# A statically planned attention and MLP kernel: a new cost model for ScalarE in its planner, new limits for DVE, and a new rule for the close of a group

## The chip, the cores and the metric

The kernel runs on one core of one Trainium2 chip. The metric is device time in microseconds (us) of one execution; lower is better.

## The reference

```python
def reference(A_x, A_wq, A_wk, A_wv, A_wo, B_x, B_w1, B_w2):
    xn = layernorm(A_x)                       # S=2048 rows, D=512, bf16
    # A: attention, 32 heads of 16 with ONE shared key and value head
    q = xn @ wq ; k = xn @ wk ; v = xn @ wv
    s = softmax(q k^T / 4) v  @ wo            # 32 x 2048 x 2048 exponentials
    # B: MLP, F=1792
    g = silu(silu(xn @ w1) @ w2)
    return A_x + s * g
```

The bulk is 134 million exponentials. One score tile is 128 keys by 512 queries of one head. Four heads and one block of 512 queries make a "group" of 64 tiles; there are 32 groups, 2048 tiles in all.

## The kernel before: the parts that matter

All instructions are laid out by a planner that runs when the program is built. It keeps one clock for each engine, gives each operation an estimated duration and a latency to whoever waits for it, and always lets the engine with the earliest clock choose what to do next. What comes out is a fixed order of instructions for each engine; on the chip each engine is given its instructions in that order, and semaphores enforce the dependencies. **So a number in the cost model never changes how long an instruction takes. It changes the order, and which engine a tile is given to.**

```python
T_P, T_SH, T_TR, T_AF = 600.0, 600.0, 630.0, 51.0   # T_AF: fixed cost of one exponential, ns
T_P64, DV_MIN, T_LIB = 1060.0, 4, 6500.0            # POOL's shift; its library
LEND_LIMIT = 3000.0
TWO_LIMIT = 1500.0
LAT = {   # ns from the end of an operation to the engine that waits
    (PE, AC): 221.0, (PE, DV): 221.0, (PE, PE): 0.0,
    (AC, PE): 402.0, (AC, DV): 390.0, (AC, AC): 250.0, ...
```

A score tile is turned into exponentials in one of two ways:

- ScalarE ("A tile"): one `activation(Exp)` over two or three PSUM banks, planned at `0.8333 * 512 * n + T_AF`. The two sets of three banks alternate, so the score matmuls for one wait until ScalarE has read it two exponentials earlier.
- DVE ("D tile"): a `tensor_scalar` writes the bits of an approximate exponential; four such tiles form a batch, of which POOL (sometimes DVE) makes three shifted copies by integer addition; all four copies are multiplied into PV. A D tile thus costs four PV matmuls, an A tile one.

At each score group the planner decides how many D tiles ride along. With one, ScalarE "lends" its third bank, and its exponential has two banks in place of three:

```python
def dve_backlog():
    return sum(t.dur for t in pl.tasks[DV] if all(p.op is not None for p in t.preds)) \
        + max(0.0, pl.clk[DV] - pl.clk[PE])
...
    bl = dve_backlog()
    want = 2 if bl < TWO_LIMIT else 1
    nd = min(cap, 4 - len(banks), len(need), want)
    if nd < min(want, len(need)) and len(banks) == 3 and bl < LEND_LIMIT:
        nd, lend = nd + 1, True
```

Between score groups TensorE does "column" work: PV rounds, and projections for queries, MLP and output ("jobs"). A round is refused if it would make the next score group late for ScalarE:

```python
    end = pe_start(t, mode) + dur + SWITCH
    if max(ts, end) > max(ts, act_need() - 437.0) + S_TOL:
        pl.clk[PE] = ts            # leave TensorE idle until the banks are free
        return True
...
def start_jobs(t):
    ...
    if jb.pace > progress() + 1e-9:                 # not ahead of its pace
        return
    if n >= NPRO and a_pressure() > (START_Z if jb.kind == "z" else START_H):
        return                                      # not while exponentials pile up for PV
...
    if pr and pr[0] == "go" and (a_pressure() >= PRESS):
        col = ("pv", pr[1])                         # PV goes first only under pressure
    elif jr[0] == "go":
        col = ("job", jr[1])
```

PV accumulates a group in one PSUM bank. When it is complete, DVE transposes the bank out ("the norm", `f_sb`), and only then may the next group's PV begin.

The softmax here doesn't subtract the row's maximum and nothing guards it: scores larger than these inputs give would overflow.

Of the kernel before, what the change touches and what calls it, by code (L numbers as in the profile page):

```python
# [5 lines left out]
ACT = mybir.ActivationFunctionType  # L6
# [11 lines left out]
LOG2E = 1.4426950408889634  # L18


T_P, T_SH, T_TR, T_AF = 600.0, 600.0, 630.0, 51.0
T_P64, DV_MIN, T_LIB = 1060.0, 4, 6500.0
RSQRT_M = float(0x5F1FFFF9)
RSQRT_C = ((-0.703952253, 0.703952253 * 2.38924456), (-0.5, 1.5))

# [9 lines left out]
PE, AC, DV, PO, SP = "PE", "ACT", "DVE", "POOL", "SP"  # L35
ENGINES = (PE, AC, DV, PO, SP)
MM = 216.0
SWITCH, SKEW = 105.0, 10.0
INF = float("inf")
DVE_LIMIT = 4000.0  # L40
MARGIN, MARGIN_END = 16, 28
LEND_LIMIT = 3000.0
TWO_LIMIT = 1500.0
HOLD, Q_LEAD = 1000.0, 3.3

LOW_USE, HIGH_USE, USE_WIN = 0.55, 0.8, 3000.0
# [2 lines left out]
NPA, PRESS = 26, 20  # L49
START_Z, START_H = 8, 14  # L50
# [6 lines left out]
class Task:  # L57
# [9 lines left out]

LAT = {
    (PE, AC): 221.0, (PE, DV): 221.0, (PE, PE): 0.0,
    (AC, PE): 402.0, (AC, DV): 390.0, (AC, AC): 250.0, (AC, PO): 410.0, (AC, SP): 410.0,  # L70
    (DV, PE): 140.0, (DV, AC): 150.0, (DV, DV): 115.0, (DV, PO): 165.0, (DV, SP): 180.0,
    (PO, PE): 120.0, (PO, AC): 120.0, (PO, DV): 120.0, (PO, PO): 90.0, (PO, SP): 120.0,
    (SP, SP): 60.0,
# [188 lines left out]
def bass_recurrent_scan__grouped_kv_mqa__dense_activation_silu__prompt_kernel(  # L262
# [19 lines left out]
    NG = 2 * NO  # L282
# [11 lines left out]
    with ExitStack() as es:  # L294
# [23 lines left out]
        t_sb = sb("t_sb", [P, 2, NQ], BF16)  # L318
# [16 lines left out]
        ps = es.enter_context(nc.psum_tensor([P, 8 * 512], FP32))  # L335
# [6 lines left out]
        def bank(b):  # L342
            return ps[:, b * 512:(b + 1) * 512]

        pl = Planner()
# [67 lines left out]
        a = 0  # L413
        for n in first:
            b = a + n
            tiles = range(a, b)
            g = a // 4
            y, w, h = rstd_sb[:, a:b], var_sb[:, 0, a:b], var_sb[:, 1, a:b]

            def dv(fn, reads, writes, pre):  # L420
                return pl.add(Task(DV, 66.0, fn, reads, writes, g, [pre] if pre is not None else []))
            t = pl.add(Task(DV, 66.0, lambda v, a=a, b=b, w=w: v.tensor_scalar(
                w, mv_sb[:, a:b, 1], LN_EPS, None, op0=ALU.add), [("mv", i) for i in tiles], [("ve", a)], g,
                [aggr[i] for i in tiles]))
            t = dv(lambda v, y=y, w=w: v.tensor_scalar(
                y.bitcast(I32), w.bitcast(I32), -0.5, RSQRT_M, op0=ALU.mult, op1=ALU.add), [("ve", a)], [("rs", a)], t)
            for it, (c0, c1) in enumerate(RSQRT_C):
                t = dv(lambda v, y=y, h=h, c0=c0: v.scalar_tensor_tensor(
                    out=h, in0=y, scalar=c0, in1=y, op0=ALU.mult, op1=ALU.mult), [("rs", a)], [("vh", a)], t)
                t = dv(lambda v, w=w, h=h: v.tensor_tensor(h, h, w, ALU.mult), [("ve", a), ("vh", a)], [("vh", a)], t)  # L430
# [8 lines left out]
            a = b  # L439
# [25 lines left out]
        def mk_T(tiles, bk=None):  # L465
            n, t0 = len(tiles), tiles[0]

            def rnd(b):
                def emit(pe, b=b):
                    dst = bank(b).bitcast(BF16).rearrange("p (t d) -> p t d", d=D)  # L470
                    h = None
                    for k, t in enumerate(tiles):
                        for dc in range(NDC):
                            h = pe.transpose(dst[:, k, dc * P:(dc + 1) * P], xn_sb[:, t % 4, dc * P:(dc + 1) * P], ident[:, :])  # L474
                    return h
                return emit

            def consume(jb, op):
                b = jb.bank
                src = bank(b).bitcast(BF16)[:, 0:n * D].rearrange("p (t c d) -> p c t d", c=NDC, d=P)  # L480
                dst = xnT_sb[:, :, t0 * P:(t0 + n) * P].rearrange("p c (t d) -> p c t d", d=P)
                keys = [("xnT", t) for t in tiles]
                if bk is not None and t0 != 1:
                    return [Task(AC, 477.0, lambda a: a.activation(dst, src, ACT.Copy), [("ps", b)], keys, 0)]
                return [Task(DV, 60.0 + 267.0 * n, lambda v: v.tensor_copy(dst, src), [("ps", b)], keys, 0)]

            job("T", tiles, 0.0, [(rnd, [("xn", t % 4) for t in tiles] + [("id", i) for i in range(4)], 4 * n * T_TP)], consume,
                preds=[xn_task[t] for t in tiles], bk=bk, mode="F")
# [84 lines left out]
        def mk_h(c, ft, pace):  # L573
            def rnd(dc):
                def mk(b):
                    return lambda pe: col4(pe, b, lambda j: w1_sb[:, dc, P * ft + 32 * j:P * ft + 32 * (j + 1)],
                                           xnT_sb[:, dc, c * NQ:(c + 1) * NQ], dc == 0, dc == NDC - 1)
                return mk

            def consume(jb, op):  # L580
                b = jb.bank
                k = tcount[0] % 2
                tcount[0] += 1
                t1 = Task(AC, 477.0, lambda a: a.activation(t_sb[:, k, :], bank(b), ACT.Tanh, scale=0.5),  # L584
                          [("ps", b)], [("t", k)], 0)
                t2 = Task(DV, T_P, lambda v: v.scalar_tensor_tensor(  # L586
                    out=u_sb[:, ft, :], in0=t_sb[:, k, :], scalar=1.0, in1=bank(b), op0=ALU.add, op1=ALU.mult),
                    [("ps", b), ("t", k)], [("u", ft)], 0, [t1])
                u_task[c, ft] = t2
                return [t1, t2]  # L590

            job("h", (c, ft), pace, [(rnd(dc), ["w1"] + xnT_keys(c), MM) for dc in range(NDC)], consume)

        def mk_z(tt, pace):
            c, r = divmod(tt, 4)

            def rnd(ft):
                def mk(b):
                    return lambda pe: col4(pe, b, lambda j: u_sb[:, ft, r * P + 32 * j:r * P + 32 * (j + 1)],
                                           w2_sb[:, ft, :], ft == 0, ft == NFT - 1)  # L600
                return mk

            def consume(jb, op):
                b = jb.bank
                k = tcount[0] % 2
                tcount[0] += 1
                t1 = Task(AC, 477.0, lambda a: a.activation(t_sb[:, k, :], bank(b), ACT.Tanh, scale=0.25),  # L607
                          [("ps", b)], [("t", k)], 0)
                t2 = Task(DV, T_P, lambda v: v.scalar_tensor_tensor(  # L609
                    out=tmp_sb[:, tt % 8, :], in0=t_sb[:, k, :], scalar=1.0, in1=bank(b), op0=ALU.add, op1=ALU.mult),  # L610
                    [("ps", b), ("t", k)], [("tmp", tt % 8)], 0, [t1])
                tmp_task[tt] = t2
                return [t1, t2]

            job("z", tt, pace, [(rnd(ft), ["w2", ("u", ft)], MM) for ft in range(NFT)], consume,
                gate=lambda: all((c, ft) in u_task and u_task[c, ft].op is not None for ft in range(NFT))
                and (tt < 8 or tt - 8 in fin_task and fin_task[tt - 8].op is not None))
# [52 lines left out]
        NPRO = len(jobs)  # L670
# [5 lines left out]
        for c in range(NC):  # L676
            base = 0.6 + span * c
            tot = 4.0 * NFT + 4 * NFT
# [25 lines left out]
        nleft = [SLOTS] * NG  # L704
# [13 lines left out]
        norm = {}  # L718
# [45 lines left out]
            return [("V", j, kt // 4)]  # L764

        def dve_backlog():
            return sum(t.dur for t in pl.tasks[DV] if all(p.op is not None for p in t.preds)) + max(0.0, pl.clk[DV] - pl.clk[PE])

        def want_d(banks_left=True):
            if st["assigned"] < 8:  # L770
# [328 lines left out]
        def progress():  # L1099
            return st["assigned"] / SLOTS  # L1100

        def start_jobs(t):
            while st["job"] < len(jobs):
                jb = jobs[st["job"]]
                n = st["job"]
                if jb.pace > progress() + 1e-9:
                    return
                if any(p.op is None for p in jb.preds):
                    return
                if jb.gate is not None and not jb.gate():  # L1110
                    return
                if n >= NPRO and a_pressure() > (START_Z if jb.kind == "z" else START_H):
                    return
                if not jb.fixed:
                    lim = 2 if n < NPRO else 1
                    if len([a for a in active if not a.fixed]) >= lim or not pool_free:
                        return
                    jb.bank = pool_free.pop(0)
                active.append(jb)
                st["job"] += 1  # L1120
# [71 lines left out]
        def a_pressure():  # L1192
            return sum(1 for b in pa_busy if b)
# [27 lines left out]
        def pe_step():  # L1221
            t = pl.clk[PE]
# [6 lines left out]
            pr = pv_round(t)  # L1229
            tr = tail_round(t)  # L1230
            col = None
            if pr and pr[0] == "go" and (a_pressure() >= PRESS):
                col = ("pv", pr[1])
            elif jr[0] == "go":
                col = ("job", jr[1])
            elif pr and pr[0] == "go":
                col = ("pv", pr[1])
            elif tr and tr[0] == "go":
                col = ("tail", None)
            elif t_done and not tail["made"]:  # L1240
                fb = fill_bank(t)
                if fb is not None:
                    col = ("fill", fb)
# [155 lines left out]
```

## Time and profile before

Median 716.68 us (3 runs, 715.52 to 717.12). In the tables PE is TensorE, ACT ScalarE, DVE VectorE, POOL GpSimd, PEld the weight loads of TensorE. `L1297` is the exponential, `L937` the D tile on DVE, `L996` POOL's shift, `L756` the score matmuls, `L1056` PV, `L458` all projections, `L1073` the norm's transpose. In the after kernel the same lines are some 2 to 12 lines further down.

The page of the kernel before: busy time of each engine, and the chain of work that ended last.

```profile
PE 669.9 (94%) x8693; PEld 191.2 (27%) x8693; DVE 604.8 (85%) x1039; ACT 676.6 (95%) x729; POOL 484.6 (68%) x472
...
ACT 79%; PE 12%; DVE 7%; issue 1%; DVEq 0%
```

ScalarE bounds it. But "95% busy" does not tell how much of that is work, since instructions overlap. The groups by shape (count, busy us, mean ns of one, idle time before them):

```profile
L1297 ACT ACTIVATE pa_sb<-ps 128x1024 bf16<-128x1024 f32 x556 | 548.2, 1229 | 4.9 <-PE ps L756 4.7
...
L937 DVE TENSOR_SCALAR db_sb<-ps 128x512 uint16<-128x512 f32 x656 | 436.4, 685 | 68.7 <-PE ps L756 62.3 <-POOL ds_sb L996 0.8
...
L1297 ACT ACTIVATE pa_sb<-ps 128x1536 bf16<-128x1536 f32 x93 | 141.8, 1602 | 8.9 <-PE ps L756 7.3 <-PE ps L1056 1.3
```

A two-bank exponential lasts 1229 ns on average, yet 556 of them fill only 548 us: each starts while its predecessor still runs. The pace has to be read from one end to the next. The timeline of ScalarE shows it where nothing waits (start, length, instruction):

```profile
213.43 0.84 ACT L584 ACTIVATE t_sb<-ps 128x512 bf16<-128x512 f32 x1
213.91 6.79 ACT L1297 ACTIVATE pa_sb<-ps 128x1024 bf16<-128x1024 f32 x7
220.28 0.91 ACT L584 ACTIVATE t_sb<-ps 128x512 bf16<-128x512 f32 x1
```

The tanh ends at 213.43 + 0.84 = 214.27, the seventh exponential at 213.91 + 6.79 = 220.70: 6.43 us for seven, 0.918 us each (0.917 with the trace's full digits). Within the seven, starts are 903 to 905 ns apart until a start lies 0.42 us before its predecessor's end, and 917 from there on; 904 is 853 + 51, the old model's fixed cost. Completions are 917 apart throughout, 853 + 64. By ends, three banks take 1344 ns and a tanh 490.

With these three numbers the whole span can be split. Every exponential and tanh gets its pace; a gap of over 40 ns beyond it is a stall; "start" is the end of the first exponential, "tail" what follows the last:

| us, profile of before | start | ScalarE at its pace | stalls to 46 us | stalls after | rest | tail | span |
|---|---|---|---|---|---|---|---|
| 556 two-bank, 93 three-bank, 656 D tiles | 16.6 | 668.7 | 7.2 | 8.5 | -0.7 | 14.7 | 715.0 |

The largest stall after the prologue is in the timeline of before around 527 to 532 us (lines of ScalarE, TensorE and DVE; in brackets the idle time before and what ended it):

```profile
527.31 0.88 ACT L1297 ACTIVATE pa_sb<-ps 128x512 bf16<-128x512 f32 x1
...
528.98 1.05 PE L458 MATMUL ps<-xnT_sb,wq_sb 128*32 128x512 bf16 x16
...
530.29 0.68 DVE L564 TENSOR_SCALAR qt_sb<-ps 128x512 bf16<-128x512 f32 x1
...
531.25 0.61 PE L756 MATMUL ps<-qt_sb,kt_sb 32*128 32x512 bf16 x6
...
531.69 1.02 ACT L1297 ACTIVATE pa_sb<-ps 128x1024 bf16<-128x1024 f32 x1 [3.50 <-PE ps L756]
```

ScalarE has run out of scores, because the queries of the next heads were projected too late. The tail, timeline of before from 698 us (`w_sb,u_sb` is the second MLP projection, 14 rounds of four matmuls):

```profile
698.40 3.19 PE L458 MATMUL ps<-w_sb,u_sb 128*32 128x512 bf16 x56
...
702.94 0.72 DVE L1073 STREAM_TRANSPOSE f_sb<-ps 128x512 f32<-128x512 f32 x1
...
703.36 3.19 PE L458 MATMUL ps<-w_sb,u_sb 128*32 128x512 bf16 x56
...
706.38 2.98 PE L458 MATMUL ps<-wo_sb,on_sb 128*32 128x512 bf16 x52
```

The last exponential ends at 700.28. TensorE is then 1.9 us into one MLP projection of 3.2 us, before the last norm, and a second whole one follows before the output projection. And TensorE is where the next limit is; the waits view of before (who waited for whom: us in total, times, longest):

```profile
PEld ps L756 <- ACT pa_sb L1297: 245.7, 531, 1.2
POOL ds_sb L996 <- PE ps L1056: 143.9, 103, 5.3
...
PEld ps L1056 <- DVE f_sb L1073: 12.8, 24, 1.6
...
PE ps L1056 <- DVE f_sb L1073: 6.3, 13, 1.3
```

The first line is mostly the usual distance between two kinds of matmul: what goes beyond it is 43 us. POOL waiting 144 us for PV to give back its buffers is a sign that PV runs late. The last two lines are PV held up by the norm.

### The profile page before, as it was taken

To read this page: it belongs to the slowest core of one execution; us is meant where nothing else is said; L and a number is where in the kernel's file an instruction comes from. 1 tells how busy PE (TensorE), PEld (TensorE's weight loads), DVE (VectorE), ACT (ScalarE), POOL (GpSimd) and SP (SyncE) were. 2 spreads that over 40 slices of the span, in tenths; PEclk is the share of its full clock that TensorE was granted. 3 is DMA by queue.
4 is the path that set the end of the run, shared out by engine and by line. 5 is a ranking of instruction groups with operands and counts; after the bars stand their busy time and mean duration, and the time that the engine had idled before them with its cause. 6 is when DMAs were issued, how large, how long until landed. Compare 5 with 4: busy or idle time off the path is not lost.

```text
span 715.0 us, 20429 instructions
## 1 busy us (share of the span) xinstructions
PE 669.9 (94%) x8693; PEld 191.2 (27%) x8693; DVE 604.8 (85%) x1039; ACT 676.6 (95%) x729; POOL 484.6 (68%) x472
## 2 busy tenths in 40 slices
PE   5799999999999999999999999998999999999996
PEld 3332222222222222222222222222232222222233
DVE  8778889989889898888887898899888898899865
ACT  3699999999999999999999999999989999999992
POOL 2037777877866777867777768778626677878780
PEclk9899999999999999999999999999999999999999
DMA  9300000000000000000000000000000000000000
GB/s 314 101 17 1 2 2 2 2 1 3 2 2 2 23 25 17 2 1 2 2 2 2 1 3 24 24 17 1 2 2 2 2 1 17 17 17 17 2 2 31
DMA packets 11434, 12.61 MB, mean 18 GB/s; under 512 B 1809, under 2 KB 10769, under 8 KB 11345
## 3 DMA queue, kind: packets, MB, share of 16 engines
q1 hardware_dynamic: 10288, 11.28, 4.9%
q8 instruction: 70, 1.15, 0.7%
q10 hardware_dynamic: 1056, 0.03, 0.1%
q14 instruction: 20, 0.16, 0.1%
HBM read 8.95 MB, written 2.10 MB: 15 GB/s over the span
## 4 chain that ended last, share of the span: by engine, by line
ACT 79%; PE 12%; DVE 7%; issue 1%; DVEq 0%
ACT pa_sb L1297 75%; PE ps L1056 4%; ACT t_sb L584 4%; PE ps L458 4%; PE ps L756 3%; DVE db_sb L937 2%; DVE ds_sb L991 1%; DVE stats_sb L405 1%; ACT t_sb L607 1%; PE ps L474 1%; DVE f_sb L1073 0%; DVE otr_sb L1077 0%; DVE xn_sb L434 0%; PE ps L500 0%; DVE fin_sb L621 0%
## 5 line engine op out<-in xcount | busy, mean ns | idle before, releaser
L1297 ACT ACTIVATE pa_sb<-ps 128x1024 bf16<-128x1024 f32 (+1 forms) x650 | 660.8, 1282 | 13.7 <-PE ps L756 12.0
L996 POOL INT64_ADD ds_sb<-db_sb x461 | 480.7, 1059 | 212.4 <-PE ps L1056 143.9
L937 DVE TENSOR_SCALAR db_sb<-ps 128x512 uint16<-128x512 f32 x656 | 436.4, 685 | 68.7 <-PE ps L756 62.3
L756 PE MATMUL ps<-qt_sb,kt_sb 32*128 32x512 bf16 x2048 | 256.1, 385 | 21.7 <-ACT pa_sb L1297 10.4
L1056 PE MATMUL ps<-ds_sb,v_sb 128*32 128x512 bf16 x1968 | 228.1, 383 | 0.9 <-DVE ds_sb L991 0.5
L1056 PE MATMUL ps<-pa_sb,v_sb 128*32 128x512 bf16 x1392 | 215.6, 384 | 0.3 <-ACT pa_sb L1297 0.3
L1056 PE MATMUL ps<-db_sb,v_sb 128*32 128x512 bf16 x656 | 154.4, 384 | 6.4 <-DVE f_sb L1073 6.3
L756 PEld LDWEIGHTS ps<-qt_sb,kt_sb 32*128 32x128 bf16 x2048 | 65.8, 91 | 305.9 <-ACT pa_sb L1297 245.7
L1056 PEld LDWEIGHTS ps<-ds_sb,v_sb 128*32 128x32 bf16 x1968 | 56.8, 95 | 55.7 <-issue 36.9
L458 PE MATMUL ps<-xnT_sb,w_sb 128*32 128x512 bf16 x896 | 69.2, 384 | 0.3 <-DVE db_sb L937 0.3
L458 PE MATMUL ps<-w_sb,u_sb 128*32 128x512 bf16 x896 | 68.5, 384 | 0.9 <-DVE db_sb L937 0.9
L1056 PEld LDWEIGHTS ps<-pa_sb,v_sb 128*32 128x32 bf16 x1392 | 54.8, 95 | 36.5 <-issue 23.3
L1056 PEld LDWEIGHTS ps<-db_sb,v_sb 128*32 128x32 bf16 x656 | 38.2, 95 | 29.8 <-DVE f_sb L1073 12.8
L584 ACT ACTIVATE t_sb<-ps 128x512 bf16<-128x512 f32 x56 | 46.0, 822 | 0.0
L586 DVE SCALAR_TENSOR_TENSOR u_sb<-t_sb,ps 128x512 bf16<-128x512 bf16 x56 | 38.1, 681 | 9.1 <-ACT t_sb L584 8.2
L991 DVE TENSOR_SCALAR ds_sb<-db_sb 128x2048 uint16<-128x2048 uint16 x31 | 26.5, 871 | 1.8 <-PE ps L1056 1.6
L458 PEld LDWEIGHTS ps<-w_sb,u_sb 128*32 128x32 bf16 x896 | 17.0, 94 | 29.3 <-issue 22.4
L1073 DVE STREAM_TRANSPOSE f_sb<-ps 128x512 f32<-128x512 f32 x32 | 22.7, 708 | 1.5 <-PE ps L1056 1.2
L458 PEld LDWEIGHTS ps<-xnT_sb,w_sb 128*32 128x32 bf16 x896 | 14.8, 94 | 27.5 <-issue 21.5
L609 DVE SCALAR_TENSOR_TENSOR tmp_sb<-t_sb,ps 128x512 bf16<-128x512 bf16 x16 | 11.0, 685 | 11.4 <-ACT t_sb L607 11.3
L458 PE MATMUL ps<-xnT_sb,wq_sb 128*32 128x512 bf16 x256 | 20.0, 399 | 0.0
L1077 DVE TENSOR_TENSOR otr_sb<-f_sb,rcp_sb 128x256 bf16<-128x256 f32 x32 | 18.7, 588 | 0.2
(54 smaller groups left out, 168.9 us busy)
## 6 DMA issues: line engine op xcount, KB each, us to landing
w_sb<-in_B_w_dram SPq DMA_DIRECT2D x2, 1792.0 KB, 13.0
xr_sb<-in_A_x_dram SPq DMA_DIRECT2D x16, 128.0 KB, 2.6
out_dram<-ob_sb SPq DMA_DIRECT2D x16, 128.0 KB, 1.7
ds_sb<-in_A_x_dram SPq DMA_DIRECT2D x3, 512.0 KB, 6.8
ds_sb<-in_A_x_dram SPq DMA_DIRECT2D x4, 128.0 KB, 2.9
wq_sb<-in_A_wq_dram SPq DMA_DIRECT2D x1, 512.0 KB, 4.8
wo_sb<-in_A_wo_dram SPq DMA_DIRECT2D x1, 512.0 KB, 15.3
kt_sb<-kt_sb SPq DMA_DIRECT2D x4, 64.0 KB, 3.4
```

The lines of the kernel that those rows point to most:

```text
L458: last = h.matmul(bank(b)[32 * j:32 * (j + 1), 0:n], lhsT=lhs(j), rhs=rhs, start=start, stop=stop, tile_position=(0, 32 * j), skip_group_c ...
L584: t1 = Task(AC, 477.0, lambda a: a.activation(t_sb[:, k, :], bank(b), ACT.Tanh, scale=0.5), [("ps", b)], [("t", k)], 0)
L586: t2 = Task(DV, T_P, lambda v: v.scalar_tensor_tensor(out=u_sb[:, ft, :], in0=t_sb[:, k, :], scalar=1.0, in1=bank(b), op0=ALU.add, op1=ALU ...
L609: t2 = Task(DV, T_P, lambda v: v.scalar_tensor_tensor(out=tmp_sb[:, tt % 8, :], in0=t_sb[:, k, :], scalar=1.0, in1=bank(b), op0=ALU.add, o ...
L756: return pe.matmul(bank(b), lhsT=kt_sb[32 * i:32 * i + 32, g % 2, kt * P:(kt + 1) * P], rhs=qt_sb[32 * i:32 * i + 32, (g // 2) % NQR, :], ...
L937: bt.P[i] = pl.add(Task(DV, T_P, lambda v, b=b, i=i, bb=bt.b: v.tensor_scalar(db_sb[:, bb, i * NQ:(i + 1) * NQ], bank(b), 128.0 * LOG2E, 1 ...
L991: whole[DV] = pl.add(Task(DV, T_SH, lambda v: v.tensor_scalar(ds_sb[:, s, :], db_sb[:, bt.b, :], SHIFT[j - 1], 1.0, op0=ALU.add, op1=ALU.m ...
L996: whole[PO] = pl.add(Task(PO, T_P64, lambda g: g.int64_add(ds_sb[:, s, :].bitcast(U64), db_sb[:, bt.b, :].bitcast(U64), words), reads, ds_ ...
L1056: h = pe.matmul(bank(OB)[32 * i:32 * (i + 1), :], lhsT=lhs, rhs=rhs, start=s0, stop=s1, tile_position=(0, 32 * i), skip_group_check=True)
L1073: t1 = pl.add(Task(DV, T_TR, lambda v: v.transpose(f_sb[:, k, :], bank(OB)), [("ps", OB)], [("F", k)], 1, [norm.get(("m", g - 2))]))
L1077: t3 = pl.add(Task(DV, 332.0, lambda v: v.tensor_tensor(o3[:, :, val:val + DH], f3[:, :, val:val + DH], rcp_sb[:, k, :].unsqueeze(2).to_br ...
L1297: op = pl.place(AC, 0.8333 * NQ * n + T_AF, lambda a: a.activation(pa_sb[:, s * NQ:(s + n) * NQ], ps[:, b0 * 512:(b0 + n) * 512], ACT.Exp) ...
```

## The change

Intent: give the planner the ScalarE pace and release that the chip shows, adjust the DVE limits to it, and at the close of a group let PV go first and let projections start early, to have work for TensorE while the norm's transpose is awaited. `closing()` below is true while the norm of the group before is not visible to TensorE, or when the group has no score tile left to hand out and at most 24 PV matmuls to go. A "gated" shift is one whose condition to start does not hold yet in the plan.

```diff
-T_P, T_SH, T_TR, T_AF = 600.0, 600.0, 630.0, 51.0
-T_P64, DV_MIN, T_LIB = 1060.0, 4, 6500.0
+T_P, T_SH, T_TR, T_AF = 600.0, 600.0, 630.0, 64.3
+T_P64, DV_MIN, T_LIB = 1035.0, 4, 300.0
+BLG = 0
+NEAR, AHEAD = 24, 0.6
-LEND_LIMIT = 3000.0
-TWO_LIMIT = 1500.0
+LEND_LIMIT = 2000.0
+TWO_LIMIT = 900.0
-    (AC, PE): 402.0, (AC, DV): 390.0, (AC, AC): 250.0, (AC, PO): 410.0, (AC, SP): 410.0,
+    (AC, PE): 157.0, (AC, DV): 140.0, (AC, AC): 110.0, (AC, PO): 160.0, (AC, SP): 160.0,
 ...   (one-bank activations: 477.0 -> 490.0, three places)
         def dve_backlog():
-            return sum(... if all(p.op is not None for p in t.preds)) + ...
+            return sum(... if all(p.op is not None for p in t.preds)
+                       and (BLG or t.gate is None or t.gate())) + ...
+        def closing():
+            g = st["gO"]
+            if g >= NG:
+                return False
+            if g > 0 and (norm.get(g - 1) is None or norm[g - 1].op is None or pl.vis(norm[g - 1].op, PE) > pl.clk[PE]):
+                return True
+            return nleft[g] == 0 and sum(tot[g, i] - done[g, i] for i in range(4)) <= NEAR
         def start_jobs(t):
 ...
-                if jb.pace > progress() + 1e-9:
+                near = n >= NPRO and closing()
+                if jb.pace > progress() + (AHEAD if near else 1e-9):
 ...
-                if n >= NPRO and a_pressure() > (START_Z if jb.kind == "z" else START_H):
+                if n >= NPRO and not near and a_pressure() > (START_Z if jb.kind == "z" else START_H):
 ...
-            if pr and pr[0] == "go" and (a_pressure() >= PRESS):
+            if pr and pr[0] == "go" and (a_pressure() >= PRESS or closing()):
```

More of the change, by code (lines that the diff above doesn't have):

```diff
@@ L483, in consume @@
                 if bk is not None and t0 != 1:
-                    return [Task(AC, 477.0, lambda a: a.activation(dst, src, ACT.Copy), [("ps", b)], keys, 0)]
+                    return [Task(AC, 490.0, lambda a: a.activation(dst, src, ACT.Copy), [("ps", b)], keys, 0)]
                 return [Task(DV, 60.0 + 267.0 * n, lambda v: v.tensor_copy(dst, src), [("ps", b)], keys, 0)]
@@ L583, in consume @@
                 tcount[0] += 1
-                t1 = Task(AC, 477.0, lambda a: a.activation(t_sb[:, k, :], bank(b), ACT.Tanh, scale=0.5),
+                t1 = Task(AC, 490.0, lambda a: a.activation(t_sb[:, k, :], bank(b), ACT.Tanh, scale=0.5),
                           [("ps", b)], [("t", k)], 0)
@@ L606, in consume @@
                 tcount[0] += 1
-                t1 = Task(AC, 477.0, lambda a: a.activation(t_sb[:, k, :], bank(b), ACT.Tanh, scale=0.25),
+                t1 = Task(AC, 490.0, lambda a: a.activation(t_sb[:, k, :], bank(b), ACT.Tanh, scale=0.25),
                           [("ps", b)], [("t", k)], 0)
@@ L766, in dve_backlog @@
         def dve_backlog():
-            return sum(t.dur for t in pl.tasks[DV] if all(p.op is not None for p in t.preds)) + max(0.0, pl.clk[DV] - pl.clk[PE])
+            return sum(t.dur for t in pl.tasks[DV] if all(p.op is not None for p in t.preds) and (BLG or t.gate is None or t.gate())) + max(0.0, pl.clk[DV] - pl.clk[PE])
         def want_d(banks_left=True):
```

## The prediction

> **What bounds the kernel now.** ScalarE. The page has it 95% busy and 79% of the chain that ended last, 75% in the exponentials. The trace's start and end times sharpen this. Between exponentials that never wait, one end follows the other by about 917 ns for two banks (128x1024), 1344 ns for three, 490 ns for a one-bank tanh. That is 0.8333 ns per column plus about 64 ns; starts are only 904 ns apart, because they queue up. (The Trainium skill, "ScalarE: Activation LUTs", section "What ACT_TABLE_LOAD costs", gives 0.833 ns per element too, but 186 ns fixed less 93 ns of overlap; the trace's 64 ns decides.) With 556 two-bank, 93 three-bank, one one-bank exponentials and 72 tanh this is a floor of about 670 us. The rest of 715 us: first exponential at 15.1 us; about 7 us of idle ScalarE in the prologue (20 to 36 us); about 8.5 us of idle in steady state, 3.6 of it at 531 us, where a query projection was placed too late and ScalarE waited for scores; and 14.7 us from the last exponential to the end, in which TensorE still does two 14-round MLP projections of 3.2 us each, left over from earlier.
>
> TensorE is close behind: it waits before score matmuls (45 to 50 us in start-to-start gaps beyond the normal switch) and about 19 us in PV for the norm's transpose (the waits view: 12.8 on weight loads, 6.3 on matmuls). DVE is 85% busy, POOL 68%.
>
> **What the change does.** No instruction is new; it only changes the order the planner emits and how many score tiles DVE takes instead of ScalarE.
> - Pace 51 to 64.3 and ScalarE release 402 to 157 ns: matches the trace (end pace 917; an exponential that did not queue lasts about 1020 to 1030 ns, TensorE starts 52 ns later: 1075 in all; the old model says 1306, the new 1075). The old plan has hardly any slack between a release and the next score group (about 65 ns), so it refuses PV and projection rounds that would fit. The new one packs TensorE better.
> - At a group's close PV goes first and projections may start early, whatever the pressure: fills the norm wait, brings query projections and MLP work forward. I expect 4 to 6 of the 8.5 us of stalls to go, and 3 to 5 us of the tail.
> - The backlog no longer counts gated shifts (600 ns each), while the limits drop to 2000 and 900. Net: "two DVE tiles" gets easier, lending about neutral. Now 656 of 2048 tiles go to DVE; I expect 660 to 690. Each moved tile saves ScalarE about 0.46 us (half of 917) and costs DVE 0.6 and POOL 0.8 us, off the critical path. Worth 2 to 14 us, I take 6: the least certain term.
> - POOL's 6.5 us library time to 0.3: the trace has 0.19 us. It frees the plan's start only; nothing.
>
> Sum: -5 stalls, -4 tail, -6 split, +1 new waits: 715 - 14 = 701 us in the profile; the measured time likewise, about 701 to 703.
>
> **Prediction: 702 us, 692 to 712 in 8 of 10.** Faster by over 2% 0.5, within 2% 0.48, slower 0.02.
>
> **Right or wrong would show:** the 3.5 us wait at the query projection gone; the norm waits of PV halved; one or no MLP projection after the last exponential; the count of DVE tiles (656) higher and of exponentials (650) lower; ScalarE still at 95%.
>
> **What would make it wrong:** the lower limits hand fewer tiles to DVE (slower, near 715); the early projections hold the one free bank and delay DVE tiles; or TensorE slack is used so well that many more tiles move (690 or below).

## The result

697.66 us median (696.7 to 700.03, 4 runs) against 716.19 (4 runs). The ratio of the two is 0.9745, 95% interval 0.9716 to 0.9775. Ratios here are the mean time of one kernel's fast runs over that of the other's in the same rounds, so not quite the ratio of the medians quoted.

The page of after:

```profile
PE 666.8 (96%) x8744; PEld 194.0 (28%) x8744; DVE 602.6 (87%) x1047; ACT 668.4 (96%) x738; POOL 511.3 (74%) x499
...
ACT 55%; PE 37%; DVE 7%; issue 1%; ACTq 0%; DVEq 0%
```

The groups of after, by shape:

```profile
L1308 ACT ACTIVATE pa_sb<-ps 128x1024 bf16<-128x1024 f32 x605 | 572.6, 1082 | 2.1 <-PE ps L758 2.0
...
L939 DVE TENSOR_SCALAR db_sb<-ps 128x512 uint16<-128x512 f32 x676 | 446.9, 684 | 66.5 <-PE ps L758 59.0 <-POOL ds_sb L998 1.3
...
L1308 ACT ACTIVATE pa_sb<-ps 128x1536 bf16<-128x1536 f32 x54 | 77.1, 1484 | 5.9 <-PE ps L758 5.9
```

There are more exponentials than before (659 against 650) and still less ScalarE work: 49 more of two banks, 39 fewer of three, so 20 tiles moved to DVE. The mean length of a two-bank exponential fell from 1229 to 1082 ns, although its pace did not change: its record overlaps less with its predecessor's. That is a trap for a reader who takes the mean length for a cost. The waits view of after:

```profile
PEld ps L758 <- ACT pa_sb L1308: 255.3, 604, 1.0
...
POOL ds_sb L998 <- PE ps L1058: 44.1, 27, 4.5
...
PEld ps L1058 <- DVE f_sb L1075: 3.6, 7, 1.0
...
PE ps L1058 <- DVE f_sb L1075: 1.9, 3, 0.7
```

POOL's wait for PV fell from 144 to 44 us, PV's wait for the norm from 19.1 to 5.5. The tail of after, timeline from 684 us:

```profile
685.47 0.40 PE L1058 MATMUL ps<-pa_sb,v_sb 128*32 128x512 bf16 x3 [0.95 <-ACT pa_sb L1308]
...
685.48 3.84 PE L460 MATMUL ps<-wo_sb,on_sb 128*32 128x512 bf16 x64
685.91 0.72 DVE L1075 STREAM_TRANSPOSE f_sb<-ps 128x512 f32<-128x512 f32 x1 [9.49 <-PE ps L1058]
```

The last exponential ends at 685.41, the last PV round follows it at once, and no MLP projection is left. The chain of waits now goes through TensorE for 37%, so the two engines are closer to balance, but ScalarE still runs at its pace for 661.7 of the 694.9 us. There is nothing to set against the stall at 531 us: after the prologue the largest single stall is 1.1 us. The same split of the span:

| us, profiles | start | ScalarE at its pace | stalls to 46 us | stalls after | rest | tail | span |
|---|---|---|---|---|---|---|---|
| before | 16.6 | 668.7 | 7.2 | 8.5 | -0.7 | 14.7 | 715.0 |
| after | 14.6 | 661.7 | 5.7 | 3.5 | -0.1 | 9.5 | 694.9 |
| difference | -2.0 | -7.0 | -1.5 | -5.0 | +0.6 | -5.2 | -20.1 |

(Two tanh of 0.5 us left the tail for the middle column; by tiles alone that column fell by 8.0. The same 1.0 us is in that column of every kernel below except `only_lib`. The first and the third column of this split hang on TensorE's clock early in the one profiled execution, as the runs on the library time show; their 3.5 us are not shown to be the change's.)

### The profile page after: what moved, and what is told of

Same layout as the page of the kernel before. It is cut to its first block, busy times and chain, and to the rows that moved or that the text cites. A ratio compares the mean times of both kernels' runs of the same rounds, so it can differ in the third digit from the quotient of the medians.

```text
span 694.9 us, 20544 instructions
## 1 busy us (share of the span) xinstructions
PE 666.8 (96%) x8744; PEld 194.0 (28%) x8744; DVE 602.6 (87%) x1047; ACT 668.4 (96%) x738; POOL 511.3 (74%) x499
## 4 chain that ended last, share of the span: by engine, by line
ACT 55%; PE 37%; DVE 7%; issue 1%; ACTq 0%; DVEq 0%
ACT pa_sb L1308 52%; PE ps L1058 15%; PE ps L758 12%; PE ps L460 10%; ACT t_sb L586 3%; DVE db_sb L939 2%; DVE stats_sb L407 1%; DVE ds_sb L993 1%; ACT t_sb L609 0%; DVE xn_sb L436 0%; DVE otr_sb L1079 0%; PE ps L476 0%; DVE xnT_sb L487 0%; ACTq L296 0%; DVE kt_sb L516 0%
## 5 line engine op out<-in xcount | busy, mean ns | idle before, releaser
L1308 ACT ACTIVATE pa_sb<-ps 128x1024 bf16<-128x1024 f32 (+1 forms) x659 | 642.2, 1115 | 8.0 <-PE ps L758 7.9
L998 POOL INT64_ADD ds_sb<-db_sb x488 | 507.3, 1057 | 166.4 <-DVE db_sb L939 122.0
L939 DVE TENSOR_SCALAR db_sb<-ps 128x512 uint16<-128x512 f32 x676 | 446.9, 684 | 66.5 <-PE ps L758 59.0
L758 PE MATMUL ps<-qt_sb,kt_sb 32*128 32x512 bf16 x2048 | 258.4, 385 | 10.4 <-ACT pa_sb L1308 6.9
L1058 PE MATMUL ps<-ds_sb,v_sb 128*32 128x512 bf16 x2028 | 261.3, 383 | 3.3 <-DVE ds_sb L993 2.5
L1058 PE MATMUL ps<-pa_sb,v_sb 128*32 128x512 bf16 x1372 | 245.9, 385 | 1.6 <-ACT pa_sb L1308 1.6
L1058 PE MATMUL ps<-db_sb,v_sb 128*32 128x512 bf16 x676 | 177.2, 384 | 1.9 <-DVE f_sb L1075 1.9
L1058 PEld LDWEIGHTS ps<-ds_sb,v_sb 128*32 128x32 bf16 x2028 | 65.0, 95 | 58.1 <-issue 34.4
L460 PE MATMUL ps<-xnT_sb,w_sb 128*32 128x512 bf16 x896 | 76.1, 384 | 0.4 <-DVE u_sb L588 0.3
L1058 PEld LDWEIGHTS ps<-db_sb,v_sb 128*32 128x32 bf16 x676 | 43.5, 94 | 23.1 <-issue 14.3
L586 ACT ACTIVATE t_sb<-ps 128x512 bf16<-128x512 f32 x56 | 37.1, 663 | 0.0
L460 PE MATMUL ps<-wo_sb,on_sb 128*32 128x512 bf16 x256 | 20.2, 383 | 0.0
## 6 DMA issues: line engine op xcount, KB each, us to landing
w_sb<-in_B_w_dram SPq DMA_DIRECT2D x2, 1792.0 KB, 13.4
```

Of the source, the lines that this page charges most:

```text
L460: last = h.matmul(bank(b)[32 * j:32 * (j + 1), 0:n], lhsT=lhs(j), rhs=rhs, start=start, stop=stop, tile_position=(0, 32 * j), skip_group_c ...
L586: t1 = Task(AC, 490.0, lambda a: a.activation(t_sb[:, k, :], bank(b), ACT.Tanh, scale=0.5), [("ps", b)], [("t", k)], 0)
L758: return pe.matmul(bank(b), lhsT=kt_sb[32 * i:32 * i + 32, g % 2, kt * P:(kt + 1) * P], rhs=qt_sb[32 * i:32 * i + 32, (g // 2) % NQR, :], ...
L939: bt.P[i] = pl.add(Task(DV, T_P, lambda v, b=b, i=i, bb=bt.b: v.tensor_scalar(db_sb[:, bb, i * NQ:(i + 1) * NQ], bank(b), 128.0 * LOG2E, 1 ...
L998: whole[PO] = pl.add(Task(PO, T_P64, lambda g: g.int64_add(ds_sb[:, s, :].bitcast(U64), db_sb[:, bt.b, :].bitcast(U64), words), reads, ds_ ...
L1058: h = pe.matmul(bank(OB)[32 * i:32 * (i + 1), :], lhsT=lhs, rhs=rhs, start=s0, stop=s1, tile_position=(0, 32 * i), skip_group_check=True)
```

## The experiments

The change has four parts: the ScalarE model ("pace": 64.3, 490 and the releases), the backlog rule and its limits, the close rule, and POOL's library time; POOL's 1035 ns was not tried by itself. Eight kernels take away one part from the new kernel, or add one part to the old. The theories: **A**, a part acts through the split of tiles alone, and the time follows from the counts in the built program; **B**, the ScalarE model acts by the order, in that TensorE is packed better; **C**, the limits make the gain and the ScalarE model does little.

All results in one table. The columns of the split are from each kernel's one profile. "TensorE late" is the idle time of TensorE before score groups after 46 us: start to start, what goes beyond 305 ns (the usual distance from another kind of matmul) or 216 (from another score matmul). All gave correct results.

| kernel | median us (range) | ratio to before | D tiles | ScalarE at its pace | stalls after 46 us | tail | TensorE late | POOL waits for PV |
|---|---|---|---|---|---|---|---|---|
| before | 716.19 (715.52-717.12) | 1 | 656 | 668.7 | 8.5 | 14.7 | 43.0 | 143.9 |
| after | 697.66 (696.7-700.03) | 0.9745 | 676 | 661.7 | 3.5 | 9.5 | 13.6 | 44.1 |
| after, old pace | 709.14 (707.71-710.21) | 0.9902 | 652 | 672.6 | 5.2 | 9.4 | 39.8 | 143.6 |
| after, old limits | 706.23 (705.13-707.51) | 0.9869 | 656 | 670.1 | 2.2 | 9.5 | 26.5 | 40.4 |
| after, no close rule | 700.88 (700.59-701.67) | 0.9795 | 672 | 663.3 | 5.2 | 9.6 | 23.1 | 81.3 |
| after, old library time | 697.93 (696.24-698.38) | 0.9748 | 676 | 661.7 | 3.6 | 9.5 | 13.6 | 44.1 |
| before, new pace | 704.43 (703.31-705.5) | 0.9843 | 656 | 669.7 | 3.6 | 9.4 | 26.7 | 42.5 |
| before, new limits | 715.12 (713.61-715.17) | 0.9986 | 660 | 668.2 | 13.0 | 10.1 | 46.3 | 151.1 |
| before, close rule | 715.05 (713.3-716.25) | 0.9990 | 648 | 674.5 | 5.8 | 9.5 | 39.4 | 145.6 |
| before, new library time | 714.55 (714.23-715.24) | 0.9986 | 656 | 668.7 | 9.9 | 14.7 | 43.3 | 145.4 |
| before, new release | 708.17 (704.68-709.84) | 0.9883 | 648 | 673.1 | 3.6 | 9.6 | 33.1 | 84.9 |
| before, new pace of 64.3 | 712.05 (710.54-712.87) | 0.9944 | 660 | 668.5 | 10.0 | 9.4 | 32.7 | 132.6 |
| after, PV not first | 706.38 (702.81-706.63) | 0.9853 | 668 | 665.0 | 6.2 | 9.6 | 22.7 | 83.2 |
| after, other limits | 692.88 (692.22-694.53) | 0.9679 | 692 | 654.8 | 6.7 | 9.4 | 14.9 | 72.7 |

(The before of the three groups of runs had medians of 715.65, 715.67 and 715.83. The expectations count one D tile more than the table where one exponential has a single bank.)

One thing no run holds fixed is the clock that TensorE was granted, which each execution records as a mean. It lies between 0.986 and 1.000, and within one kernel the slower executions mostly have the lower clock: `only_rel` took 704.68 us at 0.999 and 707.47 to 709.84 at 0.990 to 0.992; `no_lib` 696.24 at 1.000 and 697.79 to 698.38 at 0.995 to 0.997. Differences of 2 to 3 us between medians can come from this, so the main ones are also given below at like clock. Whether an order of the plan itself leads to a lower clock was not tried.

**The new kernel with the old ScalarE model** (`no_pace`)

```diff
-T_AF = 64.3   ...   (AC, PE): 157.0, (AC, DV): 140.0, ...   Task(AC, 490.0, ...)
+T_AF = 51.0   ...   (AC, PE): 402.0, (AC, DV): 390.0, ...   Task(AC, 477.0, ...)
```

> The new kernel with the old ScalarE model (51 and 477 ns, release 402). The built program has 606 two-bank and 61 three-bank exponentials and 653 tiles on DVE: a floor of 673.4 us at 917.6, 1344.3 and 490.9 ns, 10.3 above the new kernel's 663.1. Theory A (the time is start + ScalarE floor + ScalarE stalls + tail, and the pace model matters by the split it leads to): 707 to 709 us. Theory B (the pace model matters by better packing of TensorE): more than A, stalls and tail of some 5 us on top, 711 to 715. Theory C (the limits made the split and the pace model does little): 698 to 701.

709.14 us, 11.5 more than the new kernel. C is out. 10.9 us of it is ScalarE work (672.6 against 661.7), as A had it; but POOL's wait for PV and TensorE's late score groups are back at the old kernel's level, which the split does not explain. This run does not decide between A and B.

**The new kernel with the old limits** (`no_lim`)

```diff
-BLG = 0 ; LEND_LIMIT = 2000.0 ; TWO_LIMIT = 900.0
+BLG = 1 ; LEND_LIMIT = 3000.0 ; TWO_LIMIT = 1500.0
```

> The new kernel with the old backlog rule and limits (gated shifts counted, 3000, 1500). The program has 577 and 79 exponentials, 657 tiles on DVE: floor 671.0, 7.9 above. Theory A: 705 to 706 us. Theory C (limits alone make the split, and split is all): the same 705. Rival (DVE and POOL more at ease with fewer tiles, so less lost elsewhere): 700 to 702.

706.23 us, as A and C expected. The 8.6 us match the 8.4 us of added ScalarE work. At like clock the difference is 7 to 8.5 us (705.13 and 705.30 at 0.993 and 0.994, the new kernel 698.45 at 0.992 and 696.70 at 0.995). In the new kernel the limits act through the split.

**The new kernel without the close rule** (`no_close`)

```diff
         def closing():
+            return False
```

> The new kernel without the rule for the close of a group. The program has 592 and 64 exponentials, 672 tiles on DVE: floor 664.6, only 1.5 above. If the rule works by filling the norm wait and pulling projections forward (my prediction: 5 us of stalls and 4 us of tail), 705 to 708 us, with ScalarE stalls of 7 to 9 us after the prologue and projections after the last exponential. If only the split counts: 699 to 700.

700.88 us: 3.2 more, less than half of what I had expected at the least. The tail is 9.6 us as in the new kernel, so the rule is not what emptied it; the stalls come to 5.2, not 7 to 9. In the two profiles, which lie 3.9 us apart, 1.6 us are ScalarE work, 1.7 stalls after 46 us and 1.1 the start. At like clock the rule is worth 3.9 us (700.59 and 700.73 at 0.995 and 0.996, the new kernel 696.70 and 696.87 at 0.995 and 0.997).

**The new kernel with the old library time** (`no_lib`), and **the kernel before with the new one** (`only_lib`)

```diff
-T_P64, DV_MIN, T_LIB = 1035.0, 4, 300.0      # no_lib
+T_P64, DV_MIN, T_LIB = 1035.0, 4, 6500.0
-T_P64, DV_MIN, T_LIB = 1060.0, 4, 6500.0     # only_lib
+T_P64, DV_MIN, T_LIB = 1060.0, 4, 300.0
```

> The new kernel with 6500 ns for POOL's library in the plan. Same counts as the new kernel; but the program has 2 warm-up matmuls ahead of the first transposes in place of 16. If the earlier first exponential (13.1 against 15.1 us) comes from a warmer TensorE, it goes back to about 15 us and the time is 1.5 to 2.5 us more, 699 to 700, with the 16 matmuls of the first query projection taking 1.9 us in place of 1.0. If it was chance (DMA landing), the time is within 0.5 us of the new kernel's 697.7. My prediction said the library time was worth nothing.

> The kernel before with only the 300 ns library time. Counts and order as before, apart from 16 warm-up matmuls in place of 2. Warm TensorE: 1.5 to 2.5 us less, 714. Chance: 716.

The first lines of TensorE's timeline, kernel before with the new library time:

```profile
1.52 5.85 PE L1284 MATMUL ps<-zer_sb 128*128 128x512 bf16 x16 [1.52 <-DVE zer_sb L376]
...
10.73 1.04 PE L460 MATMUL ps<-xnT_sb,wq_sb 128*32 128x512 bf16 x16
```

and the new kernel with the old one:

```profile
1.52 1.03 PE L1283 MATMUL ps<-zer_sb 128*128 128x512 bf16 x2 [1.52 <-DVE zer_sb L376]
...
11.92 1.74 PE L460 MATMUL ps<-xnT_sb,wq_sb 128*32 128x512 bf16 x16
```

A third kernel, with the old library time too (`only_pace`, below):

```profile
1.52 1.03 PE L1284 MATMUL ps<-zer_sb 128*128 128x512 bf16 x2 [1.52 <-DVE zer_sb L376]
...
11.46 1.04 PE L460 MATMUL ps<-xnT_sb,wq_sb 128*32 128x512 bf16 x16
```

As long as the plan has POOL at its library, TensorE's planned clock jumps ahead and only 2 warm-up matmuls are placed in place of 16. The Trainium skill, "TensorE: Matmul & The Clock Gate", section "What's actually happening", says that TensorE runs at half its clock until it has been busy for a window of about 3.4 us. The 16 warm-ups last 5.2 to 6.2 us, and in all seven profiles with them the first query projection takes 1.03 or 1.04 us. With 2, TensorE's steady work begins at 8.2 to 8.4 us, 3.2 to 3.7 us before that projection, so close to the window that it falls on either side: 1.92 us in before and 1.74 in `no_lib`, but 1.04 to 1.17 in the other five profiles with 2. The clock records in the traces agree: the first stretch at full clock begins at 4.7 to 6.7 us with 16 warm-ups and at 10.9 to 13.9 us with 2.

In these two pairs the start moves by 1.7 to 1.8 us (14.9 against 16.6, 14.6 against 16.4). That is not the size of the effect: over all profiles the start is 14.6 to 15.7 us with 16 warm-ups and 15.3 to 16.6 with 2. The time moves by 0.1% in one case (0.9986, interval 0.9973 to 0.9999) and not to be told in the other (0.9748 against 0.9745), so both of my expectations were too large. Where the rest went differs: in the new kernel 0.8 us comes back in the stalls before 46 us (5.7 with the new library time, 4.9 with the old); in the old kernel these shrink too (7.2 to 5.9), but the stalls after 46 us grow (8.5 to 9.9), with 2.2 us of them at 497 to 499 us, at the end of a stretch at half clock.

Such stretches are what the stalls before 46 us go with. The windows view from 28 to 32 us, before and then after (the number after POOL's is the granted clock):

```profile
28.00:32.00 4.00, 4.00 (x28) 1.92 (x28) 1.71 (x4) 3.92 (x3) 0.00 (x0) 0.50 0.00 0
28.00:32.00 4.00, 3.41 (x40) 1.51 (x37) 2.48 (x6) 3.14 (x3) 0.00 (x0) 0.82 0.00 0
```

By the clock records TensorE falls back to half clock in the prologue for 6.8 us in before and five other profiles (`no_pace`, `no_lim`, `only_lim`, `only_close`, `only_taf`), whose stalls before 46 us are 6.5 to 7.2 us; for 3.4 us in after and five others, with 4.9 to 5.9 us; not at all in `only_pace` and `only_rel`, with 4.0 us. Whether the order of the plan or chance sets the length of the stretch is not shown.

**The kernel before with the new ScalarE model alone** (`only_pace`)

```diff
-T_AF = 51.0   ...   (AC, PE): 402.0, (AC, DV): 390.0, ...   Task(AC, 477.0, ...)
+T_AF = 64.3   ...   (AC, PE): 157.0, (AC, DV): 140.0, ...   Task(AC, 490.0, ...)
```

> The kernel before with only the new ScalarE model (64.3, 490, release 157). The program has the same counts as the kernel before, 556 and 93 exponentials and 657 tiles on DVE, so the floor is the same 670.6; only the order differs. Theory A (pace acts by the split alone): 716 us, unchanged. Theory B (better packing of TensorE): stalls or tail 3 to 8 us shorter, 708 to 713.

704.43 us: 11.2 us less at the same 556 and 93 exponentials and the same 656 D tiles (at a clock of 0.997 in both, 705.35 and 705.50 against 715.50 to 715.80, so some 10 us). This is the run that decides. A is refuted for the pace; B holds, and by more than it had expected. Its waits:

```profile
POOL ds_sb L998 <- PE ps L1058: 42.5, 24, 5.3
...
PEld ps L1058 <- DVE f_sb L1075: 10.4, 21, 1.1
```

POOL no longer waits for a late PV. The tail is 9.4 us with no MLP projection in it, the stalls after the prologue 3.6 us. But PV's wait for the norm is nearly what it was (10.4 against 12.8 on weight loads), so the gain did not come from there. `only_close` below cuts this wait from 19.1 to 3.1 us in all and its time does not move, though its split differs as well. Of the 13.4 us between the two profiles, 4.5 are start and prologue, where TensorE's clock differed (above); the stalls after 46 us and the tail, 10.2 us less, are what B foretold.

**The kernel before with the new limits alone** (`only_lim`)

```diff
-LEND_LIMIT = 3000.0 ; TWO_LIMIT = 1500.0 ; gated shifts counted
+LEND_LIMIT = 2000.0 ; TWO_LIMIT = 900.0  ; gated shifts not counted
```

> The kernel before with only the new backlog rule and limits. The program has 572 and 81 exponentials and 661 tiles on DVE: floor 669.1, 1.5 below. Theory A: 714 to 715 us. Theory C (limits are what gives the split its worth): 708 to 710.

715.12 us, no difference from before that the interval (0.9967 to 1.0004) shows. Four tiles move, where 20 moved in the new kernel.

**The kernel before with the close rule alone** (`only_close`)

```diff
+        def closing(): ...         (as in the change; start_jobs and pe_step use it)
```

> The kernel before with only the rule for the close of a group. The program has 613 and 58 exponentials and 648 tiles on DVE: floor 675.8, 5.2 above the kernel before. If the rule shortens stalls and tail by the predicted 9 us: 711 to 713. If only the split counts: 721.

715.05 us: nothing (0.9971 to 1.0009), and again less than I expected. In the profile stalls and tail did shrink (8.5 to 5.8, 14.7 to 9.5), 7.9 us in all, but 8 fewer tiles go to DVE, which with the two tanh costs 5.8 us of ScalarE in that column. What remains, 2 us at most, is within the spread of its runs.

**Which half of the ScalarE model: the release (`only_rel`) or the pace (`only_taf`)**

```diff
-(AC, PE): 402.0, (AC, DV): 390.0, ...        # only_rel: this alone
+(AC, PE): 157.0, (AC, DV): 140.0, ...
-T_AF = 51.0 ; Task(AC, 477.0, ...)           # only_taf: this alone
+T_AF = 64.3 ; Task(AC, 490.0, ...)
```

> The kernel before with only the shorter ScalarE release (157 ns to TensorE in place of 402, and the other ScalarE latencies), pace still 51 and 477. The program has 550 and 100 exponentials and 648 tiles on DVE: floor 674.4, 3.8 above the kernel before. If the release is what lets the plan pack TensorE (the order gave the pace model alone about 10 us at the same split), stalls, tail and score waits shrink as there and the time is 707 to 709. If the pace of 64.3 did it, 718 to 720.

> The kernel before with only the new ScalarE pace (64.3 and 490), release still 402. The program has 584 and 73 exponentials and 661 tiles on DVE: floor 669.3, 1.3 below. If the release did it: 714 to 716, with some 40 us of TensorE waits before score groups left. If the pace did it: 704 to 707.

The release alone gives 708.17, although it moves 8 tiles back to ScalarE (with the two tanh 4.4 us more in that column); the pace alone gives 712.05, with the stalls still at 10.0 and the tail mended. So the release is the larger half, and the pace alone was worth more than I had expected (714 to 716). With both, 656 tiles are on DVE, the stalls are 3.6 us and the time is 704.43.

The likely reason for the release is in the numbers of the plan (no run tests the latency to TensorE apart from ScalarE's other ones): with 402 ns, the next score group (216 ns) and its way to ScalarE (221 ns) it takes 839 of the 904 ns that the exponential in between lasts, so 65 ns are free, less than a third of a PV round of 216 ns; with 157 ns of 918, 324 ns are free. The rule shown above adds `SWITCH` (105 ns) to the round and allows `S_TOL` (30 ns): a PV round that would start just before the banks are free needs 321 ns and finds 95 in the old plan, 109 with the new pace alone, 340 with the new release alone and 354 with both. On the chip, in before, a two-bank exponential that starts after its predecessor's end lasts 1023 ns, and where TensorE waits for one it goes on 52 ns after its end (median of 531), which is the 1075 of the new model, not the 1306 of the old.

**The new kernel, PV not first** (`no_pvfirst`)

```diff
-            if pr and pr[0] == "go" and (a_pressure() >= PRESS or closing()):
+            if pr and pr[0] == "go" and (a_pressure() >= PRESS):
```

> The new kernel, but at the close of a group PV does not go ahead of projections; early projections stay. The program has 588 and 68 exponentials and 668 tiles on DVE: floor 666.3, 3.2 above. By the floor alone 701; if the missing order also costs stalls at the closes, 702 to 704. If the whole rule is worth little on its own (the kernel without it had 700.9): 700.5 to 701.5.

706.38 us, more than the upper range and 5.5 us more than with no close rule at all (ratios 0.9853 and 0.9795, other rounds). So early projections alone do harm; they need PV ahead of them. How much is less sure: its profile fell on the fastest of the four runs (702.81 at a clock of 0.997; the others 706.17 to 706.63 at 0.986 to 0.992), so the table shows only part of it: 3.3 us more ScalarE work and 2.7 us more stalls than the new kernel. At like clock the harm is 2.1 us (`no_close`: 700.73 at 0.996). The other three runs lost more at a lower clock; whether the order of this plan caused that is not shown.

**Other limits** (`better`). Runs above say that the ScalarE column is what remains, and that the limits set it once the ScalarE model is right. Many settings of the planner's limits were counted through in the plan, and one run:

```diff
-LEND_LIMIT = 2000.0 ; TWO_LIMIT = 900.0 ; MARGIN_END = 28 ; NEAR, AHEAD = 24, 0.6
+LEND_LIMIT = 2200.0 ; TWO_LIMIT = 1800.0 ; MARGIN_END = 12 ; NEAR, AHEAD = 16, 0
-START_Z, START_H = 8, 14 ; DV_MIN = 4 ; HOLD = 1000.0 ; PRESS = 20 ; CLOSING = 3
+START_Z, START_H = 6, 10 ; DV_MIN = 5 ; HOLD = 600.0 ; PRESS = 22 ; CLOSING = 4
```

> The new kernel with other limits (2200 and 1800 for the backlog, 12 for the last group's margin, projections at lower pressure and none ahead of its pace, and five smaller ones). The program has 618 and 40 exponentials and 692 tiles on DVE: floor 656.2, 6.9 below the new kernel. If the time is start, floor, stalls and tail: 690 to 692. Rival, DVE and POOL now late and ScalarE left waiting: 694 to 698, with more than 6 us of stalls after the prologue.

692.88 us, the fastest of all: 0.9679 of before, against 0.9745 for the new kernel (other rounds), so about 0.7% less than that. The groups:

```profile
L1308 ACT ACTIVATE pa_sb<-ps 128x1024 bf16<-128x1024 f32 x618 | 584.5, 1067 | 3.3 <-PE ps L758 2.5
...
L939 DVE TENSOR_SCALAR db_sb<-ps 128x512 uint16<-128x512 f32 x692 | 455.1, 683 | 59.7 <-PE ps L758 53.1 <-POOL ds_sb L998 1.4
```

The ScalarE column fell by 6.9 us, as counted, and 3.2 us of it came back as stalls (6.7 against 3.5), none of them over 0.8 us and each ended by the score matmuls. The truth is between the two expectations, and these stalls are TensorE's. Which of the changed limits brought the gain was not separated.

## Why the prediction was right, and where it was not

The time (702 predicted, 692 to 712; 697.66 measured) was in the range, and "faster by over 2%" came true, which I had given hardly more than an even chance. That the total came so near is in part luck: the sum gave the close rule 9 us and the ScalarE model no term of its own, and the runs give the close rule 3.2 us and the ScalarE model 11.2 where it was added alone. Two terms that the sum did not have, an earlier start (-2.0) and a shorter prologue stall (-1.5), are most of what it fell short by in the profile; both go with TensorE's clock in that execution, as told above. Term by term, against the profiles:

- *"-5 stalls"*: 8.5 to 3.5 us after the prologue, -5.0. The size is right, the cause I gave only in part: I put stalls and tail to the close rule. The ScalarE model alone, at an unchanged split, brings stalls to 3.6 and the tail to 9.4 us; the close rule is worth 3.2 us in the new kernel and nothing on its own.
- *"-4 tail"*: 14.7 to 9.5, -5.2. No MLP projection is left after the last exponential, as foretold. That took little: each of pace, release, limits and close rule does it when added alone (tails of 9.4 to 10.1 us).
- *"-6 split"*: 20 tiles moved, within the 660 to 690 that I gave for the new count, and the ScalarE work fell by 8.0. I laid it to the limits. Alone they move 4 tiles; with the new ScalarE model in place they are worth 8.6 us. Why a plan with the old model gives DVE so few tiles under the same limits was not tried.
- *"Library time: nothing"*: the start came 2.0 us earlier in the profile, though over all profiles the two groups overlap (14.6 to 15.7 against 15.3 to 16.6). I had looked for POOL's own time and missed that the plan's clock also decides how many warm-up matmuls are placed. In time it is worth about 1 us in the old kernel and none to be told in the new one, so the conclusion held, the reasoning did not.
- *"+1 new waits"*: +0.6 in the rest column.
- The norm wait: *halved* was right (19.1 to 5.5 us) but of no worth as a sign. The kernel before with the new pace keeps 15.4 us of it and is 11.2 us faster; the kernel before with the close rule keeps 3.1 us of it and is no faster.
- *"the count of exponentials (650) lower"* was wrong: 659. More two-bank and fewer three-bank exponentials make more instructions and less work.

The parts added one at a time give -11.2, -0.6, -0.6 and -1.1 us, 13.5 in all, and together 18.5: they are not independent. The ScalarE model has to be right first; then the limits can use the room.

## What to carry to other kernels

In a planned kernel, a wrong latency of the bounding engine can cost time though no instruction changes, because it alters what the plan dares to put in between; here 245 ns too much (402 for 157, with ScalarE's other latencies changed alike) cost some 8 us; measure it as completion to completion and as start to release in the trace, not as the length of an instruction. Split a span into start, work at pace, stalls and tail before touching it: each part of a change then shows in its own column, and compare the granted clock of the executions before laying a small difference to the change. And test parts singly and by taking them away: here the limits were worth 8.6 us in the new kernel and nothing in the old one.

## What the Trainium skill lacked or had wrong

- "ScalarE: Activation LUTs", section "What ACT_TABLE_LOAD costs": 0.833 ns per element agrees. It gives 186 ns fixed with immediate operands and an overlap of about 93 ns back to back, so 93 ns net; here completions are 917 ns apart for 1024 columns, 64 ns fixed. One that starts after its predecessor's end lasts 1023 ns, 170 fixed, so the overlap here is 106. No page that I found says that the recorded length grows while an instruction overlaps with its predecessor: 1018 to 1364 ns (before) for the same two-bank exponential, at the same pace.
- No page that I found gives the time from ScalarE's end to a waiting matmul: 52 ns in before (median of 531 waits).
- "TensorE: Matmul & The Clock Gate", section "What's actually happening": the warm-up window agrees where TensorE is busy well beyond it (16 warm-up matmuls: query projection 1.03 or 1.04 us in seven profiles); with 2 warm-ups the projection falls near its end (1.04 to 1.92 us in seven). The profile's granted clock column does not show this first warm-up: it reads 1.00 from 0 to 24 us in before as in after, although the first clock record of the trace begins at 13.9 and 5.6 us; later it does show half clock (0.50 from 28 to 32 us in before).
